# Storing the two query projections once and repeating them with step-0 reads, in a fused attention and routing kernel

## The chip, the core and the metric

The kernel runs on one core of a Trainium2 chip, as one program. The core has a matrix engine (TensorE, PE in the profile, with its weight loads as PEld), VectorE (DVE), ScalarE (ACT), GpSimd (POOL) and SyncE (SP), which here only issues DMAs. Sixteen DMA engines move data between DRAM and the on-chip memory SBUF. The metric is the device time of one execution in microseconds; the profile's span (929.5 us) is a little shorter than the time of the run it was taken from (931.37 us).

## What is computed

Two blocks follow each other. The first is an attention without softmax: queries and keys (4 batches, 4 heads, 1088 positions, 32 wide) are projected by two 8 x 32 matrices S1 and S2, and every position's 64 features are all products of the two projections.

```python
def phi(x):
    a = np.einsum('rd,bhsd->bhsr', S1, x)
    b = np.einsum('rd,bhsd->bhsr', S2, x)
    return np.einsum('bhsi,bhsj->bhsij', a, b).reshape(*x.shape[:-1], r * r)
q_p, k_p = (phi(q), phi(k))
kv = np.einsum('bhsf,bhsd->bhfd', k_p, v)
z = np.sum(k_p, axis=2)
num = np.einsum('bhsf,bhfd->bhsd', q_p, kv)
den = np.einsum('bhsf,bhf->bhs', q_p, z)[..., None] + 1e-06
return (num / den).astype(np.float32)
```

The result, laid out as x with 4352 rows and 128 columns, goes through a mixture of 8 experts: weights P for each row and expert come from 8 rounds of normalising rows and columns of exp(x w_gate), and the output is the sum over the experts of P[:, e] * (relu(x w1[e]) w2[e]), with 1024 hidden units.

## The kernel before

The expert block is by far the larger part: groups of columns of x (transposed, in `xT`) pass through `first` (L894, first product, then a relu on ScalarE at L898), sums on VectorE (L911, L956) that save multiplications, and `into` (L1067, second product). The attention lies at the start, in the first 110 us, and its work is woven into the expert work: `fill(n)` emits some steps of the expert block between the pieces of the attention. Within `tc.manual_schedule` the order of VectorE's and PE's instructions is the order in which they are written (in the first part ScalarE's too). GpSimd, SyncE, and ScalarE in the second part are ordered by a scheduler that works with estimates of durations. An engine works through its own queue in order, so an instruction that waits holds up what stands behind it; the same is true of SyncE and GpSimd when they issue DMAs.

Batch 0 makes its query features with matrices that repeat the projections on PE (`query_products`). Batches 1 to 3, which the change touches, do it with DMAs:

- `queries_ab(b)` projects the queries (L419) with `wdq`, a copy of the key projection matrix `wd` whose second half has another column order, made on GpSimd at L269 and L270. ScalarE copies the result to `qab` (L422). Each of two position halves s holds 32 rows of a and 32 rows of b: a row for each head and each of 8 features, 576 positions wide.
- SyncE stores a to the DRAM tile `qa`, every row twice (L426, two DMAs), and b to `qb`, every row eight times (L430, four DMAs). The repetition is made while writing, by a step of 0 in the source.
- `repeat_a` reads `qa` into `ph` (128 partitions of 2304 numbers) with four DMAs (L435), one for every fourth partition, so that each stored row arrives on 8 partitions in all. `repeat_b` reads `qb` into `rb`, of the same shape, with one DMA (L438).
- `times(b, c)` multiplies `ph` by `rb` on VectorE, in three thirds (L445); the product is the 64 features of the queries. `tops(b, c)` multiplies it by the keys' sums on PE (L454), `over` divides (L467, L469), and `take_over` moves the result to `xT` through DRAM (L478, L480), mostly on GpSimd's queue.

There is a single `rb`, so `repeat_b(b + 1)` is issued only after the third multiplication of batch b; `ph` has two buffers. The loads of later batches (`kx`, `qx`, `v`) and of the next expert's weights stand on the same SyncE queue behind the stores and reads. GpSimd also forms sums of the experts' weights (L200 to L203).

Of the kernel before, what the change touches and what calls it, by code (L numbers as in the profile page):

```python
# [10 lines left out]
F32 = mybir.dt.float32  # L11
# [39 lines left out]
def kernel(  # L51
# [12 lines left out]
    nc = tc.nc  # L64
    P = nc.NUM_PARTITIONS
    B, H, S, D = q.shape
    R = S1.shape[0]
# [13 lines left out]
    consts = ctx.enter_context(tc.tile_pool(name="consts", bufs=1))  # L81
# [5 lines left out]
    dram = ctx.enter_context(tc.tile_pool(name="dram", bufs=1, space=bass.MemoryType.DRAM))  # L87
# [6 lines left out]
    def bank():  # L94
        return aps.tile([P, 512], F32, tag="a", name="a")
# [31 lines left out]
    W9 = 9 * 32  # L127
# [4 lines left out]
    phs = [wk.tile([P, 2, 4 * W9], F32, name=f"ph{i}", bufs=1) for i in range(2)]  # L132
    rb = wk.tile([P, 2, 4 * W9], F32, name="rb", bufs=1)
# [113 lines left out]

    wd = consts.tile([P, 2, H, R], F32, name="wd")
    wq = consts.tile([P, 2, 2, R, R], F32, name="wq")
    wdq = consts.tile([P, 2, H * R], F32, name="wdq")  # L250

    def projections():
        flat = raw.rearrange("p n d -> p (n d)")
# [7 lines left out]
    def repeated(st):  # L261
        for s in range(2):
            one = half[:, s:s + 1].unsqueeze(2).to_broadcast([P, R, R])
            nc.vector.tensor_tensor(wq[:, 0, s], st[:, 0, 0:R].unsqueeze(2).to_broadcast([P, R, R]), one, op=Alu.mult)
            nc.vector.tensor_tensor(wq[:, 1, s], st[:, 1, 0:R].unsqueeze(1).to_broadcast([P, R, R]), one,
                                    op=Alu.mult)


        nc.gpsimd.tensor_copy(wdq[:, 0], wd[:, 0].rearrange("p h r -> p (h r)"))  # L269
        nc.gpsimd.tensor_copy(wdq[:, 1].rearrange("p (r h) -> p r h", h=H), wd[:, 1].rearrange("p h r -> p r h"))  # L270

    wdf = wd.rearrange("p n h r -> p (n h r)")
    wqf = wq.rearrange("p n h i j -> p n (h i j)")
# [11 lines left out]
    keys, queries = {}, {}  # L285
# [122 lines left out]


    def queries_ab(b):  # L410
        qa = dram.tile([H * R, 2, 2, 2 * W9], F32, name=f"qa{b}")
        qb = dram.tile([2, R, 2 * R, 2, 2 * W9], F32, name=f"qb{b}")
        ab = wk.tile([P, 3, 192], F32, tag="qab", name="qab", bufs=1)
        x = (kT if b == 1 else qT).rearrange("p (h q c t s) -> p h c t q s", h=2, q=2, c=3, t=3)
        for cs in ((0, 1), (2,)):
            pq = bank()[:, 0:192 * len(cs)].rearrange("p (c n) -> p c n", n=192)
            for i, c in enumerate(cs):
                for s in range(2):
                    nc.tensor.matmul(pq[64 * s:64 * (s + 1), i].rearrange("p (t q s) -> p t q s", t=3, q=2),  # L419
                                     wdq.rearrange("p n f -> p (n f)"), x[:, s, c], start=True, stop=True,  # L420
                                     tile_position=(0, 64 * s))
            nc.scalar.copy(ab[:, cs[0]:cs[-1] + 1], pq)  # L422
        abf = ab.rearrange("p c n -> p (c n)")
        for s in range(2):
            x = abf[64 * s:64 * s + 32].unsqueeze(1).to_broadcast([32, 2, 2 * W9])
            nc.sync.dma_start(out=qa[:, :, s], in_=x)  # L426
        for s in range(2):
            for h in range(2):
                x = abf[64 * s + 32 + h:64 * (s + 1):2].unsqueeze(1).to_broadcast([2 * R, R, 2 * W9])
                nc.sync.dma_start(out=qb[h, :, :, s].rearrange("i f n -> f i n"), in_=x)  # L430
        queries[b] = qa, qb

    def repeat_a(b):
        for j in range(4):
            nc.sync.dma_start(out=phs[b % 2][j::4], in_=queries[b][0].rearrange("(x r) j s n -> (r j) x (s n)", x=2))  # L435

    def repeat_b(b):
        nc.sync.dma_start(out=rb, in_=queries.pop(b)[1].rearrange("h i (j x) s n -> (h i j) x (s n)", x=2))  # L438

    def third(t, c):  # L440
        return t.rearrange("p i (s c n) -> p i s c n", s=2, c=3)[:, :, :, c]
# [57 lines left out]
    def attention(b):  # L499
# [13 lines left out]
        if b == 1:  # L513
            queries_ab(2)
            repeat_a(2)
        if follows:
            repeat_b(b + 1)
# [19 lines left out]
        if follows:  # L537
            keys_ab(b + 1)
            yield
            keys_products(b + 1, 0)  # L540
            if b == 1:
                transpose_q(3)
            yield
            keys_products(b + 1, 1)
            if b == 1:
                queries_ab(3)
                repeat_a(3)
            yield
            keys_products(b + 1, 2)
            yield  # L550
# [589 lines left out]
    with tc.manual_schedule(engines={engines.DVE, engines.PE, engines.Activation}):  # L1140
        st = projections()
        transpose_k(0)
        keys_ab(0)
        repeated(st)
        load_k(1)
        transpose_q(0, 0, chunks[0][1])
        query_products(0)
        for part_ in range(3):
            keys_products(0, part_)
        keys_sums(0)  # L1150
        multiply(0)
        transpose_q(0, chunks[0][1])
        keys_kept(0)
        transpose_q(1)
        query_products(1)
        fractions(0)
        multiply(1)
        queries_ab(1)
        load_q(2)
        repeat_a(1)  # L1160
        repeat_b(1)
        divide(0)
        fractions(1)
        query_products(2)
        divide(1)
# [60 lines left out]
```

## Time and profile before

| what | value |
|---|---|
| time, median of 3 runs | 932.12 us (931.32 to 932.35) |
| span of the profiled run | 929.5 us |
| DMA in the whole run | 91640 packets, 128.14 MB |
| stores of a, L426 | 6 DMAs of 144 KB, median 3.8 us to landing |
| stores of b, L430 | 12 DMAs of 288 KB, median 5.2 us to landing |
| reads of a, L435 | 12 DMAs of 288 KB, median 4.7 us to landing |
| reads of b, L438 | 3 DMAs of 1152 KB |
| multiplications, L445 | 9 of 0.94 to 0.96 us, at 34.9 to 97.6 us |
| PE busy from 110 to 930 us | 811.7 of 820 us |

In the profile, L and a number is a line of the kernel; `ph<-qa` reads "writes ph from qa". SPq and POOLq are the queues on which SyncE and GpSimd issue DMAs; a duration there is the time to issue, not to move the data. In a list of waits each line names the waiting engine, tile and line, then what ended the wait. A wait is worth something only if the engine that waits later holds up the one that is busy most, so a wait has to be followed forward to PE. Matmul ends are modelled, so the durations of neighbouring matmuls overlap.

### The profile page before, as it was taken

To read this page: it belongs to the slowest core of one execution; us is meant where nothing else is said; L and a number is where in the kernel's file an instruction comes from. 1 tells how busy PE (TensorE), PEld (TensorE's weight loads), DVE (VectorE), ACT (ScalarE), POOL (GpSimd) and SP (SyncE) were. 2 spreads that over 40 slices of the span, in tenths; PEclk is the share of its full clock that TensorE was granted. 3 is DMA by queue.
4 is the path that set the end of the run, shared out by engine and by line. 5 is a ranking of instruction groups with operands and counts; after the bars stand their busy time and mean duration, and the time that the engine had idled before them with its cause. 6 is when DMAs were issued, how large, how long until landed. Compare 5 with 4: busy or idle time off the path is not lost.

```text
span 929.5 us, 18877 instructions
## 1 busy us (share of the span) xinstructions
PE 915.1 (98%) x7434; PEld 596.6 (64%) x7434; DVE 696.7 (75%) x1200; ACT 417.5 (45%) x901; POOL 204.3 (22%) x198
## 2 busy tenths in 40 slices
PE   9999999999999999999999999999999999999997
PEld 6667544568888888875555555555555555556886
DVE  8787789896779788686976666965757977768665
ACT  2445345654444454444544444544445444445443
POOL 2021100172545502030020101101110343310220
PEclk9999999999999999999999999999999999999999
DMA  9987100222345535353444434363434555553650
GB/s 229 288 250 218 52 1 1 80 98 63 109 153 170 171 118 155 115 195 118 136 136 143 159 113 143 113 189 125 146 111 154 150 151 184 171 179 91 173 152 12
DMA packets 91640, 128.14 MB, mean 138 GB/s; under 512 B 25376, under 2 KB 69488, under 8 KB 86816
## 3 DMA queue, kind: packets, MB, share of 16 engines
q1 hardware_dynamic: 89344, 123.63, 42.9%
q0 software_dynamic: 976, 3.15, 1.1%
q8 instruction: 58, 0.95, 0.4%
q10 hardware_dynamic: 1232, 0.16, 0.1%
q14 instruction: 30, 0.25, 0.1%
HBM read 107.88 MB, written 19.05 MB: 137 GB/s over the span
## 4 chain that ended last, share of the span: by engine, by line
PE 91%; DVE 6%; issue 1%; ACT 1%; DMA 0%; SPq 0%; POOL 0%; DVEq 0%; ACTq 0%; POOLq 0%
PE a L894 49%; PE s L1067 39%; DVE hb L911 1%; PE a L336 1%; PE a L114 1%; DVE hb L956 1%; PE a L454 1%; DMA ph<-qa 0%; PE a L304 0%; ACT hb L898 0%; DVE cs L593 0%; DVE kp L320 0%; DVE kT L293 0%; DVE pqg L956 0%; PE a L488 0%
## 5 line engine op out<-in xcount | busy, mean ns | idle before, releaser
L894 PE MATMUL a<-xe,w 128*64 128x256 f32 (+1 forms) x2560 | 571.3, 470 | 0.0
L898 ACT ACTIVATE hb<-a 128x256 f32<-128x256 f32 (+4 forms) x408 | 195.3, 480 | 253.4 <-PE a L894 226.3
L894 PEld LDWEIGHTS a<-xe,w 128*64 128x64 f32 x2560 | 242.7, 137 | 76.6 <-issue 1.6
L1067 PE MATMUL s<-hb,ws 128*64 128x256 f32 (+3 forms) x1344 | 267.5, 395 | 1.8 <-DVE w L723 0.9
L898 ACT ACTIVATE hx<-a 128x256 f32<-128x256 f32 (+1 forms) x360 | 167.3, 465 | 214.5 <-PE a L894 194.7
L1067 PE MATMUL s<-hx,ws 128*64 128x256 f32 x1280 | 235.4, 379 | 0.0
L956 DVE TENSOR_TENSOR hb<-hb 128x512 f32<-128x512 f32 (+1 forms) x204 | 133.8, 666 | 95.2 <-ACT hb L898 90.3
L956 DVE TENSOR_TENSOR hx<-hx 128x512 f32<-128x512 f32 (+1 forms) x204 | 148.8, 739 | 68.0 <-ACT hx L898 63.1
L663 POOL TENSOR_TENSOR xe<-xT,xe 128x768 f32<-128x768 f32 (+2 forms) x41 | 84.8, 2070 | 501.7 <-DMA xe<-pT 405.4
L1067 PEld LDWEIGHTS s<-hb,ws 128*64 128x64 f32 x1344 | 127.8, 137 | 92.7 <-issue 63.8
L1067 PEld LDWEIGHTS s<-hx,ws 128*64 128x64 f32 x1280 | 121.2, 137 | 78.7 <-issue 59.4
L894 PE MATMUL a<-xT,w 128*64 128x416 f32 (+3 forms) x512 | 124.4, 464 | 1.3 <-DVE rd L469 0.9
L1067 PE MATMUL s<-hb,w 128*64 128x256 f32 (+3 forms) x496 | 109.6, 410 | 0.5 <-DVE kept L723 0.4
L911 DVE TENSOR_TENSOR hb<-hb 128x416 f32<-128x416 f32 (+7 forms) x96 | 68.1, 711 | 18.2 <-ACT hb L898 12.9
L1067 PE MATMUL s<-hx,w 128*64 128x256 f32 x384 | 76.5, 379 | 0.0
L894 PEld LDWEIGHTS a<-xT,w 128*64 128x64 f32 x512 | 51.8, 137 | 28.7 <-issue 11.8
L1067 PEld LDWEIGHTS s<-hb,w 128*64 128x64 f32 x496 | 50.0, 137 | 23.2 <-issue 6.8
L239 POOL TENSOR_TENSOR ws<-w 128x256 f32<-128x256 f32 (+1 forms) x70 | 59.4, 883 | 12.8 <-PE a L894 9.8
L911 DVE TENSOR_TENSOR hx<-hx 128x256 f32<-128x256 f32 (+1 forms) x65 | 38.8, 602 | 24.6 <-ACT hx L898 20.8
L956 DVE TENSOR_TENSOR pqg<-hb 128x512 f32<-128x512 f32 x68 | 47.5, 739 | 0.0
L1067 PEld LDWEIGHTS s<-hx,w 128*64 128x64 f32 x384 | 38.6, 137 | 8.5
L956 DVE TENSOR_TENSOR pqg<-hx 128x512 f32<-128x512 f32 x68 | 36.4, 574 | 0.0
(170 smaller groups left out, 477.6 us busy)
## 6 DMA issues: line engine op xcount, KB each, us to landing
w<-in_moe_w_dram SPq DMA_DIRECT2D x82, 512.0 KB, 5.6
ws<-ws SPq DMA_DIRECT2D x34, 1024.0 KB, 5.0
xe<-pT SPq DMA_DIRECT2D x34, 384.0 KB, 4.1
ws<-ws SPq DMA_DIRECT2D x12, 512.0 KB, 3.7
qb<-qab SPq DMA_DIRECT2D x12, 288.0 KB, 5.2
ph<-qa SPq DMA_DIRECT2D x12, 288.0 KB, 4.7
rb<-qb SPq DMA_DIRECT2D x3, 1152.0 KB
pb<-pT SPq DMA_DIRECT2D x6, 384.0 KB, 7.4
```

Of the source, the lines that this page charges most:

```text
L114: nc.tensor.matmul(warm[:, 0:P], ones, ones, start=True, stop=True)
L239: tc.keep_in_program_order(nc.gpsimd.tensor_tensor(ws[:, c:c + len(ns)], blocks(x), blocks(y), op=Alu.subtract if off else Alu.add))
L336: nc.tensor.matmul(pv[64 * s:64 * (s + 1), i], kp[0:n, H * t + h].rearrange("p i j -> p (i j)"), vx[0:n, slots[h], t, :], start=(t == 0 an ...
L454: nc.tensor.matmul(pn[64 * s:64 * (s + 1), t, 2 * i:2 * i + 2].rearrange("p h d -> p (h d)"), ph[:, i, s, 64 * t:64 * (t + 1)], kvs[b % 2] ...
L663: tc.keep_in_program_order(nc.gpsimd.tensor_tensor(out, x, pb, op=Alu.mult))
L894: nc.tensor.matmul(ph[sl], loaded_w[j][0][:, P * f + H2 * s:P * f + H2 * (s + 1)], sources[j][:, lo:hi], start=True, stop=True, tile_posit ...
L898: nc.scalar.activation(out=out, in_=ph, func=Act.Relu)
L911: nc.vector.tensor_tensor(out, a, b, op=Alu.subtract)
L956: nc.vector.tensor_tensor(out if not isinstance(out, tuple) else places(*out), places(*a), places(*b) if isinstance(b, tuple) else b, op=A ...
L1067: nc.tensor.matmul(sums[g][i][H2 * s:H2 * (s + 1), n * place:n * (place + 1)], w, x, start=c == 1, stop=c == per, tile_position=(0, H2 * s))
```

## The change

a and b are each stored once: four DMAs of 72 KB a batch, for the two halves s and for a and b. The repetition moves to the reads, where a step of 0 in the DRAM source names each row eight times. a is then read by a single DMA with 128 rows of 9216 bytes. b needs its rows repeated in another order (the whole block of 8 rows, eight times over), for each of two pairs of heads, so it is read by two DMAs of 64 partitions, one on SyncE's queue and one on GpSimd's. With b stored in the plain order the second column order isn't needed, so `wdq` and its two copies go, and L419 uses `wd` itself. The purpose is to write and store fewer bytes, to issue fewer DMAs from SyncE, and to have the two halves of b issued by two engines.

```diff
--- before.py
+++ after.py
@@ -247,7 +247,6 @@
 
     wd = consts.tile([P, 2, H, R], F32, name="wd")
     wq = consts.tile([P, 2, 2, R, R], F32, name="wq")
-    wdq = consts.tile([P, 2, H * R], F32, name="wdq")
 
     def projections():
         flat = raw.rearrange("p n d -> p (n d)")
@@ -264,10 +263,6 @@
             nc.vector.tensor_tensor(wq[:, 0, s], st[:, 0, 0:R].unsqueeze(2).to_broadcast([P, R, R]), one, op=Alu.mult)
             nc.vector.tensor_tensor(wq[:, 1, s], st[:, 1, 0:R].unsqueeze(1).to_broadcast([P, R, R]), one,
                                     op=Alu.mult)
-        nc.gpsimd.tensor_copy(wdq[:, 0], wd[:, 0].rearrange("p h r -> p (h r)"))
-        nc.gpsimd.tensor_copy(wdq[:, 1].rearrange("p (r h) -> p r h", h=H), wd[:, 1].rearrange("p h r -> p r h"))
 
     wdf = wd.rearrange("p n h r -> p (n h r)")
     wqf = wq.rearrange("p n h i j -> p n (h i j)")
@@ -408,8 +403,7 @@
 
 
     def queries_ab(b):
-        qa = dram.tile([H * R, 2, 2, 2 * W9], F32, name=f"qa{b}")
-        qb = dram.tile([2, R, 2 * R, 2, 2 * W9], F32, name=f"qb{b}")
+        ds = [dram.tile([2 * R, 2, 2, 2 * W9], F32, name=f"q{n}{b}") for n in "ab"]
         ab = wk.tile([P, 3, 192], F32, tag="qab", name="qab", bufs=1)
         x = (kT if b == 1 else qT).rearrange("p (h q c t s) -> p h c t q s", h=2, q=2, c=3, t=3)
         for cs in ((0, 1), (2,)):
@@ -417,25 +411,26 @@
             for i, c in enumerate(cs):
                 for s in range(2):
                     nc.tensor.matmul(pq[64 * s:64 * (s + 1), i].rearrange("p (t q s) -> p t q s", t=3, q=2),
-                                     wdq.rearrange("p n f -> p (n f)"), x[:, s, c], start=True, stop=True,
+                                     wdf, x[:, s, c], start=True, stop=True,
                                      tile_position=(0, 64 * s))
             nc.scalar.copy(ab[:, cs[0]:cs[-1] + 1], pq)
         abf = ab.rearrange("p c n -> p (c n)")
         for s in range(2):
-            x = abf[64 * s:64 * s + 32].unsqueeze(1).to_broadcast([32, 2, 2 * W9])
-            nc.sync.dma_start(out=qa[:, :, s], in_=x)
-        for s in range(2):
-            for h in range(2):
-                x = abf[64 * s + 32 + h:64 * (s + 1):2].unsqueeze(1).to_broadcast([2 * R, R, 2 * W9])
-                nc.sync.dma_start(out=qb[h, :, :, s].rearrange("i f n -> f i n"), in_=x)
-        queries[b] = qa, qb
+            for n, d in enumerate(ds):
+                lo = 64 * s + 32 * n
+                nc.sync.dma_start(out=d[:, :, s].rearrange("r x n -> x r n"), in_=abf[lo:lo + 32])
+        queries[b] = ds
 
     def repeat_a(b):
-        for j in range(4):
-            nc.sync.dma_start(out=phs[b % 2][j::4], in_=queries[b][0].rearrange("(x r) j s n -> (r j) x (s n)", x=2))
+        rows = queries[b][0].rearrange("r x s n -> r (x s n)")
+        nc.sync.dma_start(out=phs[b % 2], in_=rows.unsqueeze(1).to_broadcast([2 * R, R, 8 * W9]))
 
     def repeat_b(b):
-        nc.sync.dma_start(out=rb, in_=queries.pop(b)[1].rearrange("h i (j x) s n -> (h i j) x (s n)", x=2))
+        rows = queries.pop(b)[1].rearrange("r x s n -> r (x s n)")
+        for h, queue in enumerate((nc.sync, nc.gpsimd)):
+            queue.dma_start(out=rb[64 * h:64 * (h + 1)],
+                            in_=rows[R * h:R * (h + 1)].unsqueeze(0).to_broadcast([R, R, 8 * W9]))
 
     def third(t, c):
         return t.rearrange("p i (s c n) -> p i s c n", s=2, c=3)[:, :, :, c]
```

## The prediction

> **What bounds the kernel now.** First the page's busy table, because it says which engine a change must reach.
>
> ```profile
> span 929.5 us, 18877 instructions
> PE 915.1 (98%) x7434; PEld 596.6 (64%) x7434; DVE 696.7 (75%) x1200; ACT 417.5 (45%) x901; POOL 204.3 (22%) x198
> ```
>
> PE is idle for 929.5 - 915.1 = 14.4 us. Busy is not peak, but the matmuls' number, shapes and order on PE are fixed by hand and the change keeps them, so it can act only through idle PE time. Next, the stages in which batches 1 to 3 use the edited lines (18 to 110 us), from the view of busy time by stretch.
>
> ```profile
> core 0: us, PE busy (x) PEld busy (x) DVE busy (x) ACT busy (x) POOL busy (x), PEclk, DMA share, GB/s
> 18.00:42.00 24.00, 23.27 (x284) 15.21 (x280) 19.46 (x36) 9.27 (x25) 1.29 (x6) 1.00 0.99 297
> 42.00:68.00 26.00, 23.86 (x317) 16.60 (x316) 21.33 (x39) 12.36 (x35) 6.49 (x9) 1.00 0.86 247
> 68.00:110.00 42.00, 40.19 (x485) 27.49 (x487) 33.72 (x62) 18.25 (x45) 5.67 (x10) 1.00 0.50 145
> ```
>
> The DMA engines are full (0.99) while batch 1 is repeated, which makes the change tempting. But PE is idle there for only 0.73 + 2.14 + 1.81 = 4.7 us, and that is the most a speed-up here can return. What ended those gaps is in PE's waits between 16 and 110 us (columns: total us, times, longest).
>
> ```profile
> PE a L894 <- DVE rd L469: 0.9, 1, 0.9
> PE a L304 <- DVE kT L295: 0.8, 1, 0.8
> PE a L454 <- DVE rd L469: 0.8, 1, 0.8
> PE a L454 <- issue: 0.6, 1, 0.6
> PE a L454 <- ACT m L735: 0.6, 1, 0.6
> PE s L1067 <- DVE hb L911: 0.3, 1, 0.3
> PE a L894 <- DVE xT L403: 0.2, 1, 0.2
> PE a L454 <- ACT hb L898: 0.2, 1, 0.2
> ```
>
> No DMA is named. It could act through VectorE, so I asked the timelines of VectorE and PE what follows the one wait for `rb` (start, duration, then the idle time before and its releaser).
>
> ```profile
> 34.92 0.96 DVE L445 TENSOR_TENSOR ph<-ph,rb 128x768 f32<-128x768 f32 x1 [1.72 <-DMA rb<-qb]
> 37.10 0.69 DVE L911 TENSOR_TENSOR hb<-hb 128x512 f32<-128x512 f32 x1 [1.23 <-ACT hb L898]
> 38.16 0.92 PE L454 MATMUL a<-kvs,ph 128*64 128x66 f32 x24 [0.25 <-ACT hb L898]
> ```
>
> VectorE waits 1.72 us for `rb`, multiplies until 35.88, and then sits idle 1.23 us for ScalarE. Its next work starts at 37.10 whether the multiply started at 33.2 or 34.9. PE reads the product at 38.16, released by ScalarE. So the wait is absorbed before it reaches PE; equally, `rb` may come about 1.2 us later (multiply at 36.1) before anything moves. In batches 2 and 3 the first multiply starts at 62.27 and 89.89 without a wait.
>
> Last, the SyncE queue of batch 1:
>
> ```profile
> 17.96 1.27 SPq L426 DMA_DIRECT2D qa<-qab  x2
> 19.29 3.60 SPq L430 DMA_DIRECT2D qb<-qab  x4
> 22.98 1.29 SPq L166 DMA_DIRECT2D qx<-in_q_dram  x1
> 24.38 3.11 SPq L435 DMA_DIRECT2D ph<-qa  x4
> 27.60 1.04 SPq L438 DMA_DIRECT2D rb<-qb  x1
> ```
>
> Issuing is what takes the time from 18 to 28: 1.27 + 3.60 + 3.11 + 1.04 = 9.0 us.
>
> [...] (1) [...] The new stores have a slowest dimension of 2 (x) and the halves of b a leading step-0 dimension of 8[...] The trace has a GpSimd DMA of that size (xd<-xt), which landed 4.2 and 8.8 us after issue beside other traffic; I use those.
>
> **The change part by part.**
>
> *The removed copies (L269, L270).* 0.21 + 0.23 us of GpSimd at 5.8 us, which next waits 10.07 us for a weight load. Worth nothing. The projections (L419) take `wdf` in place of `wdq`: the same 36 matmuls of 326 ns.
>
> *Stores.* Per batch six DMAs (2 x 144 + 4 x 288 = 1440 KB) become four of 72 KB (288 KB). At about 0.6 us of issue each (qa: 592 ns) they take 2.4 us of SyncE instead of 4.9. Their landing is what the trace can't show. Lower bound: issued by 20.4, landed after 3.6 us as qa: 24.0. Upper bound: two engines. The best slices of the DMA view move about 424 GB/s, 26.5 GB/s an engine, so 295 KB need 5.6 us on two. Batch 1's kx, issued at 13.35 with up to 8.5 us to landing, stands ahead until about 21.9: landed at 27.5.
>
> *Reads of a.* Four DMAs of 288 KB become one of 1152 KB: the same bytes, 3.1 us of issue becoming 0.6 to 1.3.
>
> *Reads of b.* One DMA of 1152 KB becomes two of 576 KB, one issued by GpSimd at an estimated 0.6 to 0.7 us (xd<-xt: 561 to 729 ns). GpSimd has nothing between 19.3 and 44.7, so its new wait for the stores holds up nobody in batch 1. In batch 2 the weight sums (44.73 to 48.4) or the half may go first; the first matmul of that expert is at 59.3. In batch 3 it stands between the xT stores (end 66.1) and the next xd (84.03), in free time.
>
> *When b lands in batch 1.* a and b together are 2.36 MB. Lower bound, all 16 engines: 24.0 + 2.36 MB / 424 GB/s = 29.6[...], so 31.6. Upper bound, both halves on the same eight engines: each moves 74 KB of a and 147 KB of b, 221 KB / 26.5 GB/s = 8.3 us, so 27.5 + 8.3 + 2 = 37.8. The first gives back the 1.72 us wait, hidden as shown: 0. The second starts the multiply 1.7 us after the free 36.1: +1.7 us. I take the middle, about 34.7, practically today's 34.9: cost 0, because few things make both restrictions and the backlog meet.
>
> *Batches 2 and 3, upper bound.* Batch 2's stores start at 42.45 behind weights that end at 44.7: 44.7 + 5.6 + 8.3 + 2 = 60.6, before 62.27. Batch 3: 68.68 + 5.6 + 8.3 + 2 = 84.6, before 89.89. Both 0; the kx and v loads behind them start earlier and had time to spare (VectorE waited 0.2 us in all for kx).
>
> *Sum.* Bytes fall by 3 x 1152 KB = 3.5 MB of 128 MB, SyncE issue by some 5 us a batch, and PE gets nothing: 932.12 + 0 = 932.1.
>
> **The rivals.**
>
> *A: the relief reaches PE (faster).* For: DMA share 0.99, and VectorE's wait is the longest for the edited tiles. Against: 1.23 us of idleness directly after it, and no DMA among PE's waits. If all of it did pass on, with the 0.8 us gap of L454 at 42.81 that follows in VectorE's chain: 1.72 + 0.81 = 2.5, so 929.6; with all gaps of the stage 932.1 - 4.7 = 927.4.
>
> *B: b arrives late, through few engines or the second queue (slower).* For: the shapes in (1), and a GpSimd DMA that took 8.8 us. Against: 12 us of room in batch 3 and the absence of other GpSimd work. If stores landed at 27.5, a's read kept SyncE busy 1 us and a half took 8.8 us with two more for traffic, b would come at 39.3: 3.2 us late, with 0.3 for a wait the multiply now has on two DMAs: 935.6.
>
> *C: the upper bound alone,* +1.7: 933.8, still inside 0.2%.
>
> **How the numbers follow.** Forecast (no change, including C's part that costs under 1.86 us): 0.53. A: 0.25; it stands that high because ScalarE and GpSimd are not ordered by hand in the second part, and small shifts there could close gaps I count as fixed. B: 0.22. The bound of 0.2% is 1.86 us, so faster 0.25, same 0.53, slower 0.22. Range: down to 928.5 takes in A's central case, up to 935.8 takes in B's and C; left out are A's extreme and a longer stall, under 0.2 together.
>
> **What would show it.** Right: about 3.5 MB less DMA, SyncE's issue for batch 1 ending near 26 or 29 instead of 28.6, the multiply at L445 starting before 36.1, hb L911 next to it unmoved against PE, and idle PE from 18 to 110 us within 1 us of 4.7. Wrong on A's side: those gaps fall below 3 us. Wrong on B's: a wait of L445 for `rb` over 3 us, or a PE gap at L454 released by VectorE's ph or by a DMA. A reordering of ScalarE work that lengthens gaps elsewhere would make the forecast wrong for a reason I haven't priced.

## The result and the profile after

The changed kernel takes 945.38 us (944.15 to 948.29, 4 runs) against 931.72 us before: a ratio of 1.0153, with an interval of 1.0127 to 1.0179. It is slower by about 13.7 us.

The page's busy table of the changed kernel:

```profile
span 942.3 us, 18863 instructions
PE 919.2 (98%) x7434; PEld 591.4 (63%) x7434; DVE 694.3 (74%) x1200; ACT 417.6 (44%) x901; POOL 202.4 (21%) x199
```

The span grew by 12.8 us. PE's idle time grew from 14.4 to 942.3 - 919.2 = 23.1 us, that is by 8.7, and PE's busy time by 919.2 - 915.1 = 4.1 us, with the same 7434 matmuls. Both need an explanation. Busy time by stretch, in the columns and stretches used for before:

```profile
18.00:42.00 24.00, 19.48 (x228) 12.18 (x224) 13.72 (x28) 8.16 (x22) 1.69 (x6) 0.98 0.73 171
42.00:68.00 26.00, 21.34 (x253) 15.89 (x255) 20.27 (x36) 10.03 (x27) 4.54 (x6) 0.82 0.61 168
68.00:110.00 42.00, 37.38 (x485) 27.85 (x483) 28.85 (x52) 17.55 (x45) 5.59 (x10) 0.92 0.58 158
```

Idle PE in this stage is now 4.52 + 4.66 + 4.62 = 13.8 us instead of 4.7, and the clock column, which was 1.00, shows 0.82 and 0.92. The DMA columns are the other surprise: share and GB/s have both fallen from 18 to 68 us, although VectorE now waits for DMAs. What ended PE's waits, 16 to 110 us:

```profile
PE a L449 <- issue: 12.2, 3, 8.1
PE a L889 <- DVE rd L464: 0.5, 1, 0.5
PE a L299 <- DVE kT L290: 0.5, 1, 0.5
PE a L889 <- DVE xT L398: 0.3, 1, 0.3
```

L449 is `tops` (L454 before). "issue" says that the view found no releaser, so the timelines must name it. VectorE, then PE:

```profile
44.20 0.96 DVE L440 TENSOR_TENSOR ph<-ph,rb 128x768 f32<-128x768 f32 x1 [10.91 <-DMA rb<-qb]
45.08 0.68 DVE L906 TENSOR_TENSOR hb<-hb 128x512 f32<-128x512 f32 x1
45.79 0.23 DVE L347 COPY kvs<-a 64x66 f32<-64x66 f32 x1
```

```profile
46.12 1.59 PE L449 MATMUL a<-kvs,ph 128*64 128x66 f32 x24 [8.12 <-issue]
```

VectorE waits 10.91 us for `rb`, then at once does what had stood behind the multiply, the copy of the keys' sums among it, and PE starts 0.1 us after that copy. The multiply starts 9.3 us later than before; about 1.2 us of that is absorbed as before, and the other 8.1 reach PE. SyncE's queue in batch 1:

```profile
18.01 0.75 SPq L421 DMA_DIRECT2D qa<-qab  x1
...
20.08 0.58 SPq L421 DMA_DIRECT2D qb<-qab  x1
20.76 0.37 SPq L166 DMA_DIRECT2D qx<-in_q_dram  x1
25.06 0.58 SPq L427 DMA_DIRECT2D ph<-qa  x1
27.20 0.63 SPq L432 DMA_DIRECT2D rb<-qb  x1
```

Issuing is shorter, as intended, but SyncE now waits for the stores to land (21.1 to 25.1, and again before 27.20), so `rb` is issued 0.4 us earlier than before, and the multiply that waits for it starts 9.3 us later. Busy PE and clock (seventh column) around the gap:

```profile
38.00:44.00 6.00, 0.00 (x1) 0.00 (x0) 0.00 (x0) 0.02 (x1) 0.00 (x0) 0.74 0.51 158
44.00:50.00 6.00, 3.88 (x39) 2.94 (x41) 5.67 (x9) 0.41 (x1) 0.00 (x0) 0.50 0.91 241
50.00:56.00 6.00, 6.00 (x74) 4.80 (x72) 2.95 (x7) 2.82 (x8) 2.75 (x4) 0.90 0.28 79
```

PE comes out of its wait at half speed (0.50). And while nothing else runs, from 38 to 44 us, the DMA share is 0.51 with both halves of b outstanding: about what eight engines of sixteen give. Not all of it is b: by the packets its rows are 97 of the 158 GB/s, and the rest are loads that were issued behind it.

### The profile page after: what moved, and what is told of

Its sections match the earlier page's. It is cut to its first block, busy times and chain, and to the rows that moved or that the text cites. A ratio compares the mean times of both kernels' runs of the same rounds, so it can differ in the third digit from the quotient of the medians.

```text
span 942.3 us, 18863 instructions
## 1 busy us (share of the span) xinstructions
PE 919.2 (98%) x7434; PEld 591.4 (63%) x7434; DVE 694.3 (74%) x1200; ACT 417.6 (44%) x901; POOL 202.4 (21%) x199
## 2 busy tenths in 40 slices
DMA packets 89528, 124.60 MB, mean 132 GB/s; under 512 B 25184, under 2 KB 69296, under 8 KB 84320
## 4 chain that ended last, share of the span: by engine, by line
PE 91%; DVE 6%; issue 2%; ACT 1%; POOL 0%; DVEq 0%; ACTq 0%; POOLq 0%
PE a L889 48%; PE s L1062 40%; DVE hb L906 1%; PE a L331 1%; PE a L114 1%; PE a L449 1%; DVE hx L906 0%; PE a L299 0%; DVE cs L588 0%; DVE kp L315 0%; DVE kT L288 0%; DVE rd L464 0%; ACT hb L893 0%; PE a L413 0%; PE a L483 0%
## 5 line engine op out<-in xcount | busy, mean ns | idle before, releaser
L889 PE MATMUL a<-xe,w 128*64 128x256 f32 (+1 forms) x2560 | 525.7, 470 | 0.0
L889 PEld LDWEIGHTS a<-xe,w 128*64 128x64 f32 x2560 | 222.8, 137 | 64.4 <-issue 0.4
L1062 PE MATMUL s<-hb,ws 128*64 128x256 f32 (+3 forms) x1344 | 243.9, 396 | 0.9 <-DVE w L718 0.9
L1062 PE MATMUL s<-hx,ws 128*64 128x256 f32 x1280 | 208.2, 379 | 0.0
L951 DVE TENSOR_TENSOR hx<-hx 128x512 f32<-128x512 f32 (+1 forms) x204 | 154.4, 767 | 68.8 <-ACT hx L893 64.0
L1062 PEld LDWEIGHTS s<-hb,ws 128*64 128x64 f32 x1344 | 122.7, 138 | 99.8 <-issue 75.3
L1062 PEld LDWEIGHTS s<-hx,ws 128*64 128x64 f32 x1280 | 113.8, 137 | 90.9 <-issue 69.2
L889 PE MATMUL a<-xT,w 128*64 128x416 f32 (+3 forms) x512 | 127.3, 473 | 1.1 <-DVE rd L464 0.5
L1062 PE MATMUL s<-hb,w 128*64 128x256 f32 (+3 forms) x496 | 104.2, 413 | 0.4 <-DVE kept L718 0.4
L906 DVE TENSOR_TENSOR hb<-hb 128x416 f32<-128x416 f32 (+7 forms) x96 | 65.9, 688 | 20.5 <-ACT hb L893 11.0
L1062 PE MATMUL s<-hx,w 128*64 128x256 f32 x384 | 69.3, 379 | 0.1
L239 POOL TENSOR_TENSOR ws<-w 128x256 f32<-128x256 f32 (+1 forms) x70 | 58.5, 870 | 13.8 <-PE a L889 9.6
```

The lines of the kernel that those rows point to most:

```text
L239: tc.keep_in_program_order(nc.gpsimd.tensor_tensor(ws[:, c:c + len(ns)], blocks(x), blocks(y), op=Alu.subtract if off else Alu.add))
L889: nc.tensor.matmul(ph[sl], loaded_w[j][0][:, P * f + H2 * s:P * f + H2 * (s + 1)], sources[j][:, lo:hi], start=True, stop=True, tile_posit ...
L906: nc.vector.tensor_tensor(out, a, b, op=Alu.subtract)
L951: nc.vector.tensor_tensor(out if not isinstance(out, tuple) else places(*out), places(*a), places(*b) if isinstance(b, tuple) else b, op=A ...
L1062: nc.tensor.matmul(sums[g][i][H2 * s:H2 * (s + 1), n * place:n * (place + 1)], w, x, start=c == 1, stop=c == per, tile_position=(0, H2 * s))
```

## The experiments

Three theories stood against each other. Theory 1: the shape of b's read leaves it too few DMA engines. Theory 2: the half on GpSimd's queue is late. Theory 3: reading the same DRAM rows eight times is slow by itself. Edits are against the kernel named; in a diff, `...` stands for lines left out. Beside these runs the kernel before took 930.85 to 931.86 us. The form of a DMA is the list of its dimensions, the slowest first; I count two dimensions as merged into one where no gap lies between the rows. "Pace" below is taken from the trace's records of DMA packets, which give start, duration and size: the rows of `rb`, and of `ph` where it is read by one DMA, are the packets of 9216 bytes. I use batch 3, where other traffic is low: in the stretches shown below these rows make up nearly all that is moved.

| kernel | time us | ratio and interval | first multiply, batch 1, us |
|---|---|---|---|
| changed | 945.38 | 1.0153 (1.0127 to 1.0179) | 44.20 |
| a_only | 937.77 | 1.0078 (1.0061 to 1.0095) | 39.30 |
| b_only | 941.48 | 1.0108 (1.0092 to 1.0123) | 41.91 |
| halves_sync | 948.72 | 1.0191 (1.0176 to 1.0206) | 45.65 |
| stores16 | 945.93 | 1.0158 (1.0143 to 1.0174) | 41.79 |
| b_eight_engines | 945.98 | 1.0161 (1.0139 to 1.0184) | 45.74 |
| b_halves_merged | 935.16 | 1.0044 (1.0030 to 1.0058) | 40.20 |
| spread_rows | 945.23 | 1.0157 (1.0142 to 1.0172) | 43.86 |
| shifted | 945.59 | 1.0151 (1.0125 to 1.0177) | 44.59 |
| b_quarters | 947.35 | 1.0164 (1.0147 to 1.0180) | 42.92 |
| b_sixteenths | 937.27 | 1.0054 (1.0037 to 1.0071) | 43.01 |
| a_gaps | 946.31 | 1.0167 (1.0115 to 1.0219) | 43.40 |
| a_merged | 944.36 | 1.0134 (1.0105 to 1.0163) | 43.27 |
| warm | 942.11 | 1.0125 (1.0109 to 1.0141) | 44.12 |
| after_pair | 946.33 | 1.0162 (1.0147 to 1.0176) | 44.66 |
| warm_pair | 941.27 | 1.0111 (1.0097 to 1.0126) | 43.60 |

### Which part costs: a alone, b alone

a_only, against before:

```diff
-        for j in range(4):
-            nc.sync.dma_start(out=phs[b % 2][j::4], in_=queries[b][0].rearrange("(x r) j s n -> (r j) x (s n)", x=2))
+        rows = queries[b][0].rearrange("r x s n -> r (x s n)")
+        nc.sync.dma_start(out=phs[b % 2], in_=rows.unsqueeze(1).to_broadcast([2 * R, R, 8 * W9]))
```

with a stored once as in the change; b_only has the opposite half of the change.

> Only a is changed (two stores of 72 KB, one step-0 read); b is stored eight times and read by one DMA of 128 distinct rows, as before. Theory 1 (b's read runs on too few engines): no loss, 932 +- 2, the multiply of batch 1 starts at 33 to 35. Theory 2 (b's second half on GpSimd's queue starts late and shares with later loads): the same, 932 +- 2. Theory 3 (a step-0 read is slow because the same DRAM rows are read eight times): a's read takes some 10 us to landing instead of 5, b stands behind it, multiply of batch 1 at 37 to 39, time 934 to 938.

> Only b is changed (two stores of 72 KB, step-0 read in two halves, one on SyncE's and one on GpSimd's queue); a as before. Theories 1 and 2: nearly the whole loss, 941 to 946, multiply of batch 1 at 42 to 45. Theory 3: about half of it, 936 to 941, since half the step-0 reads are gone.

Both cost: 0.78% and 1.08%. In a_only a's 128 rows took 6.1 us in batch 3, the b rows behind them 4.9, so theory 3 gained ground: a's read is slow, although all sixteen engines are busy with it (DMA share 1.00 at 218 GB/s, 81 to 84 us). The profiled run of a_only was its shortest (933.15 at a granted clock of 1.000; the others 936.95 to 938.71 at 0.994 to 0.995), so the multiply's time in the table may be early for a usual one. b_only, at 941.48, is at the lower edge of what theories 1 and 2 expected: 1.08 of 1.53%, about 70% of the loss rather than nearly all. The two parts add up to 1.86%, more than the whole, so they are not independent of each other.

### Whose queue

halves_sync, against the changed kernel:

```diff
-        for h, queue in enumerate((nc.sync, nc.gpsimd)):
+        for h, queue in enumerate((nc.sync, nc.sync)):
```

> The changed kernel with both halves of b issued by SyncE, one after the other. Theory 1: still eight engines for all of b, so b lands no earlier than 41 and the time is 941 to 946. Theory 2: [...] the multiply of batch 1 starts at 37 or before and the time is 932 to 936. Theory 3: 942 to 946.

948.72, no better and rather worse, so theory 2 is not what costs most. With both halves on one queue b's rows took 11.1 us in batch 3, against 8.0 on two queues (9.1 in after_pair, a second profile of the changed kernel). In batch 1 of the changed kernel the two halves ended together, at 42.9 and 43.0. In batch 2 the second queue does cost something, because GpSimd's half stands behind `xd<-xt`, a store of `take_over`. GpSimd's queue:

```profile
63.54 0.60 POOL L473 DMA_DIRECT2D xd<-xt  x1 [6.93 <-DVE kept L715]
64.14 0.58 POOL L432 DMA_DIRECT2D rb<-qb  x1
```

SyncE had issued its half at 62.02. By the packets GpSimd's half ended 1.2 us after SyncE's (75.66 and 74.46), and in after_pair 5.4 us after it (78.44 and 73.05).

### The stores' engines

stores16, against the changed kernel:

```diff
-                nc.sync.dma_start(out=d[:, :, s].rearrange("r x n -> x r n"), in_=abf[lo:lo + 32])
+                for x in range(2):
+                    nc.sync.dma_start(out=d[:, x, s], in_=abf[lo + 16 * x:lo + 16 * (x + 1)])
```

> The changed kernel with each store split in two of 16 rows by 576, whose slowest dimension is 16[...]; eight stores a batch instead of four, the same bytes. If the stores' two engines matter: the stores of b have landed by 25 instead of 27.2, everything after is some 2 us earlier and the time is 940 to 943. If they don't (theories 2 and 3, or the later loads set the pace): 944 to 947.

The stores of the changed kernel do run on two engines. Its DMA view from 20.5 to 25.0 us, in 40 slices (first line the busy share in tenths):

```profile
DMA  1120111113299329895998689665311211111120
GB/s 61 61 41 0 61 61 41 41 41 61 20 232 193 98 118 312 314 466 234 389 546 307 234 330 546 273 273 157 121 41 41 100 61 41 41 61 62 41 41 0
```

Outside the burst in the middle, a `qx` load, the share is 1 tenth (2 of 16 is 0.125) at 41 to 61 GB/s; by the packets of 2304 bytes, two were in flight at once for 6.9 of the 7.4 us of batch 1's stores. With the stores split `rb` was issued at 23.3 instead of 27.2, and the first multiply of batch 1 moved from 44.20 to 41.79. But that of batch 2 was at 77.05 (76.45 in the changed kernel), and the time did not change. What took the gain back in batch 2 was GpSimd's half, which again stood behind `xd<-xt`; SyncE's queue, then GpSimd's:

```profile
55.41 0.61 SPq L433 DMA_DIRECT2D rb<-qb  x1
61.42 0.58 POOL L433 DMA_DIRECT2D rb<-qb  x1
```

By the packets SyncE's half ended at 67.7 and GpSimd's at 76.3. So this run does not show that the stores' two engines cost nothing; on how many engines the split stores ran was not measured, and split stores with both halves of b on SyncE's queue were not tried.

### Distinct rows on eight engines, and the same split on sixteen

b_eight_engines, against before (the stores leave a gap after each block of 8 rows, so that the dimensions can't merge):

```diff
-        nc.sync.dma_start(out=rb, in_=queries.pop(b)[1].rearrange("h i (j x) s n -> (h i j) x (s n)", x=2))
+        qb = queries.pop(b)[1]
+        for h in range(2):
+            nc.sync.dma_start(out=rb[64 * h:64 * (h + 1)],
+                              in_=qb[h, :, 0:2 * R].rearrange("i (j x) s n -> i j (x s n)", x=2))
```

b_halves_merged splits the same way without gaps: each half is 64 x 2304.

> The kernel before, with one thing changed: b, stored eight times as before but with a gap after every block of 8 rows, is read in two halves by SyncE in the form 8 blocks x 8 rows x 2304, so that its slowest dimension is 8; all 128 rows are still distinct in DRAM. If eight engines are the cause by themselves: the 128 rows take 8 to 10 us instead of 3.9, multiply of batch 1 at 39 to 42, time 936 to 942. If the step-0 reads of the same rows are the cause: 128 rows in about 5.6 us (eight engines at the 347 ns per row of before), multiply at 35.5 to 37, time 931 to 934.

> The kernel before, with b's 128 distinct rows read in two DMAs of 64 partitions, without gaps, so that each can run on 16 engines (form 64 x 2304). If the form [...] is what cost 15 us with eight engines: b's rows in about 4 to 5 us, multiply of batch 1 at 35 to 37, time 930 to 933. If splitting b in two DMAs was to blame: 938 to 946.

This is the experiment that decides. With every row distinct, b_eight_engines costs 1.61%, as much as the whole change, and more than either theory had forecast. The fair partner for its pace is halves_sync, which reads b in the same form and on the same queue, but each row eight times: 11.1 us in batch 3 against 10.3, so repeating the rows costs some 0.8 us here and the form the rest. Of the 1.61% the split into halves is 0.44% (935.16, above my 930 to 933), and the form 8 x 8 x 2304 the rest. b's rows in batch 3: 10.3 us in b_eight_engines, 6.9 in b_halves_merged, 4.9 before. Theory 1 wins, but not as I had put it, because neither figure fits a count of engines (eight and sixteen, by the DMA shares of 0.52 and 1.02 shown further down): eight at the 347 ns a row of before would need 5.6 us. The packets show why. Their median is 347 ns before, 608 in b_eight_engines and 656 in b_halves_merged: an engine is slowed, not only missing.

### Does it matter that rows are read again?

```diff
-        ds = [dram.tile([2 * R, 2, 2, 2 * W9], F32, name=f"q{n}{b}") for n in "ab"]
+        ds = [dram.tile([2 * R, R, 8 * W9], F32, name=f"q{n}{b}")[:, 0].rearrange("r (x s n) -> r x s n", x=2, s=2)
+              for n in "ab"]
```

is spread_rows, against the changed kernel. shifted differs from the changed kernel in the source of b alone:

```diff
-                            in_=rows[R * h:R * (h + 1)].unsqueeze(0).to_broadcast([R, R, 8 * W9]))
+                            in_=AP(tensor=rows.tensor, offset=rows.offset, ap=[[8 * W9, R], [8 * W9, R], [1, 8 * W9]]))
```

> The changed kernel, with the stored rows of a and b 73728 bytes apart in DRAM instead of 9216, so that they lie in as large a region as the eight copies of before. If the step-0 reads are slow because so few bytes of DRAM hold all that is read: rows fall from 550 to 690 ns to near 347, b lands by 37, time 932 to 936. If it is the same row being read again and again, wherever it lies, or the engine count: 943 to 947 as the changed kernel.

> The changed kernel with another choice of rows in the reads of b: block i of the eight reads rows i to i + 7 instead of rows 0 to 7 each time (so b holds wrong rows and the output isn't the reference's). Same form, same eight engines, same bytes, still rows read several times over[...]. If engines that read one row at the same time hold each other up: the 128 rows take 6 to 7 us instead of 10 to 15, time 934 to 939. If not (the engine count or repeated reading as such): 943 to 947.

Neither moved: 945.23 and 945.59, and in batch 3 b's rows took 9.5 and 7.6 us (8.0 and 9.1 in the two profiles of the changed kernel). How far apart the rows lie in DRAM, and which rows a block reads, makes no difference that shows here. a settles the rest. a_gaps and a_merged store a eight times and read it by one DMA of distinct rows. They differ in a gap, and so in the form. a_gaps, against before; a_merged has `R + 0` for `R + 1`, and `(r j)` for `r j` in the read:

```diff
+        qa = dram.tile([2 * R, R + 1, 2, 2, 2 * W9], F32, name=f"qa{b}")
...
+                nc.sync.dma_start(out=qa[:, 0:R, x, s], in_=y)
...
+        nc.sync.dma_start(out=phs[b % 2], in_=queries[b][0][:, 0:R].rearrange("r j x s n -> r j (x s n)"))
```

> The kernel before, with a stored eight times (four stores of 288 KB, like b's) with a gap after each block of 8 rows, so that one read of a, 128 distinct rows of 9216 bytes, keeps the form 16 x 8 x 2304 that the step-0 read of the changed kernel has. If the form makes a's read slow [...]: a's 128 rows take 5 to 6 us (about 25 a us), as with only a changed, time 934 to 939. If reading the same rows eight times made it slow: 3.5 to 4 us (about 40 a us), 931 to 934.

> As the one with gaps after a's blocks, without the gaps: the same stores and bytes, but the read's dimensions merge to 128 x 2304. Both theories: a's 128 rows in 3.5 to 4 us and the time of the kernel before plus at most 2 us for the larger stores, 931 to 934. If it is as slow as the one with gaps, neither the form nor the repetition is the cause, but the 9216-byte rows or the larger stores.

The times say little, as the larger stores put off `rb` to 31.8 and 32.5 us; the times that I expected were wrong for both. The pace is what they were for, and it came as expected for the form: in batch 3 a's rows took 5.8 us in a_gaps and 3.7 in a_merged. The stretch of batch 3 in which a is read, in a_gaps, and in a_merged:

```profile
91.00:95.00 4.00, 3.19 (x49) 2.18 (x47) 3.87 (x9) 1.57 (x4) 0.21 (x1) 1.00 1.00 237
```

```profile
96.00:101.00 5.00, 4.19 (x57) 2.86 (x55) 4.82 (x11) 2.07 (x5) 0.33 (x1) 1.00 1.02 418
```

All engines are busy in both (1.00 and 1.02), but they move 237 GB/s in the form 16 x 8 and 418 merged (the second stretch includes b, which is merged too). The step-0 read in a_only moved 218 from 81 to 84 us and took 6.1 us in all. So the form, not the repetition, slows a: theory 3 falls too.

### The same rows in four DMAs and in eight

What slows an engine isn't shown by the runs so far. Two more split b's distinct rows in other ways: b_quarters reads them in four DMAs, 8 x 4 x 2304 on 32 partitions, b_sixteenths in eight DMAs of 16 partitions. b_quarters, with b stored with a gap after every 4 rows (the stores are left out here), then b_sixteenths, both against before:

```diff
-        nc.sync.dma_start(out=rb, in_=queries.pop(b)[1].rearrange("h i (j x) s n -> (h i j) x (s n)", x=2))
+        qb = queries.pop(b)[1]
+        for p in range(0, P, 32):
+            h, i = p // 64, p % 64 // 8
+            nc.sync.dma_start(out=rb[p:p + 32],
+                              in_=qb[h, i:i + 4, :, 0:R].rearrange("i g (j x) s n -> (i g) j (x s n)", x=2))
```

```diff
-        nc.sync.dma_start(out=rb, in_=queries.pop(b)[1].rearrange("h i (j x) s n -> (h i j) x (s n)", x=2))
+        rows = queries.pop(b)[1].rearrange("h i (j x) s n -> (h i j) (x s n)", x=2)
+        for p in range(0, P, 16):
+            nc.sync.dma_start(out=rb[p:p + 16], in_=rows[p:p + 16])
```

> The kernel before, with b's distinct rows read in four DMAs of 32 partitions, each in the form 8 x 4 x 2304 (a gap after every 4 rows), so that still only eight engines read b[...] 128 rows in 5.6 to 6.5 us (23 a us, packets of 347 ns), multiply of batch 1 at 37 to 39 (the split stores and reads take some 4 us more to issue), time 932 to 937. If eight engines are slow by themselves: 10 to 13 us as in two halves, 942 to 947.

> The kernel before, with b's distinct rows read in eight DMAs of 16 partitions each, which run on 16 engines, one row an engine[...] 128 rows in 8 to 11 us, multiply of batch 1 at 39 to 43, time 936 to 944. If only the number of engines matters: 128 rows in about 4 to 5 us, multiply at 35 to 38 (4 us more to issue), 931 to 935.

Batch 3 of b_eight_engines, then of b_quarters, then of b_halves_merged, while b is read:

```profile
94.00:101.00 7.00, 6.33 (x94) 4.79 (x93) 6.75 (x15) 2.51 (x7) 0.54 (x1) 1.00 0.52 133
```

```profile
97.00:101.00 4.00, 3.19 (x49) 2.42 (x50) 3.90 (x9) 1.49 (x4) 0.56 (x1) 1.00 0.53 202
```

```profile
86.00:90.00 4.00, 3.46 (x52) 2.82 (x54) 3.90 (x9) 1.50 (x4) 0.56 (x1) 1.00 1.02 212
```

The first two have the share of eight engines (0.52 and 0.53) and move 133 and 202 GB/s; in b_quarters the median packet of batch 3 is back at 347 ns, so eight engines as such don't lengthen the packets. The third has all sixteen and moves 212. The number of engines alone does not order the runs: eight move 133 or 202 by the form, sixteen 212, 237 (a_gaps) or 418 (a_merged). All 128 rows took 10.3, 7.4 and 6.9 us in the three runs; for b_quarters I had expected 5.6 to 6.5 with packets of 347 ns and 10 to 13 from eight engines that are slow by themselves.

b_sixteenths has sixteen busy engines too (a share of 1.06 from 88 to 92 us), packets of 687 ns and 227 GB/s, about the pace of b_halves_merged. One thing does not fit: when the halves in form 8 x 8 come from two queues, the eight engines moved 184 GB/s in batch 3 of the changed kernel (92 to 96 us, share 0.52), but 131 in b_only (87 to 95), so something beside the form has a part in the pace. Which engine serves which partition isn't in the trace; why an engine is slower in one form than in another is not shown.

In time b_quarters did not profit (947.35): eight stores of b and four reads take longer to issue (6.86 and 2.83 us against 3.60 and 1.04 before), `rb` began at 30.0, and its rows took 8.9 us in batch 1 and 11.2 in batch 2, with loads behind them. Its expected 932 to 937 was wrong, and the argument rests on the pace in batch 3 alone. b_sixteenths at 937.27 fell in the higher of its two ranges, 936 to 944, but its eight reads also took 11.43 us to issue, so its time decides nothing.

### What the waiting does to PE's clock

warm and warm_pair, against the changed kernel, in `tops` (after_pair is the changed kernel itself):

```diff
+        if c == 0 and b < 3:
+            for _ in range({1: 36, 2: 14}[b]):
+                nc.tensor.matmul(pn.rearrange("p t h d -> p (t h d)")[:, 0:P], ones, ones, start=True, stop=True)
```

> The changed kernel with matmuls of ones put in front of the first use of the product, 36 in batch 1 and 14 in batch 2, which is work for about the time that PE waits there; they are overwritten. If the time lost beyond PE's gaps (12.8 us of span against 8.7 us of added idleness) is the lowered PE clock after the wait (0.50 granted from 44 to 50 us): the clock stays at 1.00 and the time is 940 to 943. If the clock is not the reason: 945 to 949, since the matmuls can only be in the way.

> The changed kernel as it is, as the partner of the filled one on the same chip: 944 to 947.

> The changed kernel with the matmuls of ones in PE's waits (36 in batch 1, 14 in batch 2). If the lowered clock is a part of the loss: 2 to 4 us less than its partner, clock 0.999. If it is none: the same as its partner or more.

The interval of warm overlaps that of the changed kernel. Those of warm_pair and its partner after_pair don't: 946.33 became 941.27, 5.1 us less, by adding work. From 38 to 50 us in warm_pair:

```profile
38.00:44.00 6.00, 6.00 (x54) 5.99 (x54) 0.40 (x1) 0.10 (x1) 0.00 (x0) 1.00 0.49 165
44.00:50.00 6.00, 6.00 (x77) 4.87 (x76) 5.84 (x10) 1.00 (x3) 0.00 (x0) 1.00 0.97 283
```

The clock stays at 1.00. Not all of the 5.1 us is the clock, though. With the added matmuls GpSimd issues its half of b in batch 2 ahead of `xd<-xt` (60.45) instead of behind it (64.46 in after_pair), and PE waits 3.2 us for that product instead of 6.3. A fairer pair of profiles is that of the changed kernel shown above, where PE waited 8.12 and 3.54 us, and that of warm_pair, where the product came 8.2 and 3.2 us after PE's last other work: the spans are 942.3 and 938.7, so some 3.3 us of difference are left, which is an estimate from one profile of each. PE's busy time had grown by 4.1. So a quarter to a third of the loss is the slow restart after PE's waits. In the changed kernel the clock falls while PE waits: PE's last work ends at 38.00, and the clock shows 1.00 from 40.50 to 40.90 us and 0.53 from 40.90 to 41.30, so it fell 2.9 us into the gap. It shows 0.50 from 46.12, where PE starts again, to 51.10 and 1.00 from 51.20 to 56.00, so it stayed low for some 5.0 us of work. In the gap of 3.54 us it shows 1.00 from 76.10 to 78.40 and 0.50 from 78.50 to 79.60; PE starts again at 79.67, and the clock shows 0.50 from 79.70 to 85.20 and 1.00 from 85.40 to 90.00.

No run beat the kernel before. Faster transfers in this stage could have returned at most the 4.7 us for which PE is idle there, and no DMA was among the releasers of those gaps.

## Why the prediction was wrong, by its steps

- *What bounds the kernel, and the slack.* The slack was right. By the prediction each us of the multiply past 36.1 costs one: 44.20 - 36.1 = 8.1, and PE's gap is 8.12 us. That the change can act only through idle PE time was wrong; see the clock below.
- *Bytes, copies and issue.* Right: 128.14 to 124.60 MB, 3.5 MB less, and SyncE's last issue for batch 1 ends at 27.83, between 26 and 29.
- *Stores.* The upper bound held: two engines, the second wait over at 27.20 against 27.5. That the two agree so well is partly luck: by the packets the stores ran from 19.4 to 26.9, so they began before the assumed 21.9 and took 7.5 us instead of 5.6. In batch 1 this term cost 2.4 us (stores16); over the whole kernel its worth stays open.
- *Reads, upper bound.* This is the term that was mis-sized. I put a and b at 8.3 us on eight engines, at 26.5 GB/s each, plus 2 us; by the packets their rows ran from 26.4 to 43.0, 16.6 us. a's 128 rows took 6.2 us where sixteen engines at full rate need 2.8 (1.18 MB at 424 GB/s), and b's 10.8. The number of engines was an assumption, and it held: eight for b (a share of 0.50 from 90.7 to 96 us), sixteen for a (1.00 in a_only). The speed of an engine I took from slices in which the merged read of before ran; in the new forms an engine was slower, with median packets of 694 ns for a and 626 for b against 347. The rate per engine measured in one form did not carry over to another. The loads issued behind b were not in the sum either: in batch 3, where there are few, b took 8.0. The 2 us at the end of each sum were my estimate; in batch 1 from the last row to the multiply that waits for it there were 0.4 us before (34.54 to 34.92) and 1.2 in the changed kernel (43.03 to 44.20).
- *The choice of the middle.* Wrong in kind. I wrote that few things make both restrictions and the backlog meet; but the two restrictions are not chances that must coincide, they came with the shapes (the stores at a share of 1 tenth in batch 1, b at 0.51 and 0.50 in batches 1 and 3). With the upper bound, not the middle, as the estimate I would have had 933.8 for batch 1, still too low.
- *Batches 2 and 3.* Batch 3 came out right, with no wait for b, but by luck: its last row arrived at 96.8 instead of by 84.6, and the multiply had itself slid to 103.26. Batch 2 was wrong, for a reason I could have read off the order of PE's work: the projections of batch 2 (L413) stand behind the waiting `tops`, so batch 2's stores start at 52.84 instead of 42.45 and take the delay along. The mis-sized reads add to it (13.6 us by the packets, 62.1 to 75.7), and so does GpSimd's half, which came last. The multiply is at 76.45 after 5.36 us of wait, and PE has a second gap of 3.54 us.
- *The clock.* Not in the sum at all. PE's busy time grew by 4.1 us at half speed; the added matmuls took 5.1 us back, of which some 3.3 by the clock.
- *The rivals.* B had the direction and half the reason: few engines. Its other half, the GpSimd queue, was wrong for batch 1, where both halves end together, and right in part for batch 2, where GpSimd's half ends 1.2 us after the other (5.4 in after_pair). Its 935.6 fell short because it stopped at one delay of 3.2 us. Nothing of A was seen.

Batch 2 in the changed kernel, VectorE and then PE:

```profile
76.45 0.96 DVE L440 TENSOR_TENSOR ph<-ph,rb 128x768 f32<-128x768 f32 x1 [5.36 <-DMA rb<-qb]
79.67 1.59 PE L449 MATMUL a<-kvs,ph 128*64 128x66 f32 x24 [3.54 <-issue]
```

The delays add up in the trace: the first multiply of batch 3 comes at 103.26 instead of 89.89, 13.4 us later, and the span is 12.8 us longer.

## What to carry to other kernels

A transfer that is hidden has a deadline, and a change that makes it smaller can still make it later: write down when the consumer's slack ends and hold the new transfer's worst time against it. In these runs that time followed the form of the transfer and not its bytes: a's 128 rows took 3.7 us merged and 5.8 as 16 x 8 x 2304, b's 6.9 in two halves of 64 x 2304 and 10.3 as two of 8 x 8 x 2304. When an engine may be held up, look at what stands behind it in its own queue, because that is how a delay gets into the next stage (batch 2's stores started at 52.84 us instead of 42.45 here), and count a slow restart of PE for a gap (after those of 8.12 and 3.54 us here its clock stayed at 0.50 for 5.0 and 5.5 us of work).

## What the hardware showed that I had not expected

- Reads of 128 rows of 9216 bytes moved 418 GB/s merged to 128 x 2304 and 237 in the form 16 x 8 x 2304, with all sixteen engines busy in both.
- 36 and 14 useless matmuls in PE's waits made the kernel 5.1 us faster, some 3.3 of it by the clock.
- SyncE can be held up while issuing: the eight DMAs of b in b_sixteenths took 11.43 us to issue (27.30 to 38.73), where the four of a just before took 3.08. What holds it isn't in the trace.
